# One store per output block, transfers gated on other transfers, and a planner that models the load queue: a change to a fused attention and feed-forward kernel

## The chip, the cores and the metric

The kernel runs on one core of one Trainium2 chip. The time is the device time of one execution in microseconds, and I quote the median of several executions with the lowest and the highest. A profile is one such execution with every instruction recorded. TensorE does the matmuls, VectorE, ScalarE and GpSimd the work between them, and SyncE does nothing here but hand transfers to the DMA engines: "the queue" below is the line of transfers that SyncE hands over, in the order of its list. A weight load and a matmul overlap (in the kernel before they are busy for 153.9 and 218.2 us of a span of 232.9), and the busy time of an engine is time in which at least one of its instructions is recorded.

## The reference

Attention over 4 batches of 768 tokens with 8 heads of 64 (a local band of 96 keys and 8 global keys, a distance bias and a softmax), and a feed-forward on its 3072 x 512 result.

```python
scores = scale * np.matmul(q, k.transpose(0, 1, 3, 2))       # q, k, v: (4, 8, 768, 64) f32
keep = is_global | is_local                                  # 8 global keys, 96 local ones
scores = np.where(keep, scores + bias[None, :, :, :], -1e9)
a = softmax(scores)                                          # shortened
x = np.matmul(a, v).transpose(0, 2, 1, 3).reshape(3072, 512)
h = x @ w_in                                                 # 512 x 2048
g = np.maximum(h, 0.0) + np.log1p(np.exp(-np.abs(h)))        # softplus
out = g @ w_out                                              # 2048 x 512
```

## The kernel before

The 3072 tokens are 24 blocks of 128, in 12 windows of 256. A window is loaded, cast to bf16, and transposed for the scores. Each block gives an attention result `xs`, which is transposed into `XT`. A group of the feed-forward is one window: its first layer (`mm1`) needs the `XT` of both its blocks, ScalarE computes exp and then ln (softplus) into `g`, and its second layer (`mm2`) sums into `o_ps`, is copied to an output buffer `osb` by VectorE and stored.

Every operation is given to a small planner. It simulates the engines with the durations written in the code and fixes the order of the instructions on each engine before the kernel is built. An engine then runs its list in order, whatever really happens: in the trace of the kernel before, VectorE stands 6.06 us before a cast that starts at 101.02, and the copy behind it in the list, whose matmuls started at 97.39 and took 1.04 us, starts at 102.78.

The layout of tokens is where the change begins. A partition p of a loaded tile holds the tokens 2p and 2p+1, so that its two tokens are one piece of 512 bytes in each head. A block therefore comes out with its even tokens first and its odd ones after. The store has to put that right:

```python
def store(g, ns):
    osb = state["osb", g, ns]
    t0 = W * g + P * ns
    dst = out[t0 : t0 + P, :].rearrange("(p r) c -> r p c", r=2)
    for r in range(2):
        nc.sync.dma_start(dst[r], osb[64 * r : 64 * r + 64, :])      # even rows, odd rows

def softplus_ln(g, c):
    gt = tile_of(ffn, ("g", g), [P, NFB, W], BF16)
    nc.scalar.activation(
        gt[:, 4 * c : 4 * c + 4, :].rearrange("p a t -> p (a t)"),
        state["e", g, c][:].rearrange("p a t -> p (a t)"),
        AF.Ln,
        bias=1.0,
    )
```

The first transfers are held back by gates, so that what is needed first gets the DMA engines: a gate is a tiny copy that reads the last bytes of an earlier transfer. Loads of windows 4 and later wait for a matmul group instead.

```python
    load_rest(1, -180.0)
    gate = pool_gate(1, -171.0)          # GpSimd: after k of window 1
    add_weights(0, -170.0, gate)         # w_in and w_out, first quarter
    add_weights(1, -169.0, gate)
    chain = sp_gate(1, -160.0)           # queue: after the second quarter of w_in
    load_rest(2, -150.0)
    gate = pool_gate(2, -149.1)
    add_weights(2, -149.0, gate)
    add_weights(3, -148.0, gate)
    chain = sp_gate(3, -145.0)           # queue: after the fourth quarter of w_in
    for w in range(3, NWIN):
        load_rest(w, base(2 * w) - 14.0)
    # ... cut ...
    for w in range(4, NWIN):
        for what, p in (("q", 0), ("k", 0), ("v", 2)):
            for o in loaded[w, what]:
                o.wait_for(mm1s[w - 3, p])
```

The first blocks are transposed into `XT` by TensorE, the others by a transposing DMA on the same queue:

```python
        if n < 6 or n // 2 == NGRP - 1:
            t = pl.add(f"TX{n}", "pe", 0.23, lambda op: x_transp(n, tr_bank(op.taken)), ...)
            # ... the copy out of PSUM, on VectorE or ScalarE
        else:
            xdone[n] = pl.add(f"DX{n}", "sp", 1.2, lambda op: x_dma(n), u - 20.0, ...)
```

The softmax here doesn't subtract the row's maximum and nothing guards it: scores larger than these inputs give would overflow.

## Time and profile before

| | before |
|---|---|
| time | 232.75 us (231.75 to 233.35, the 3 runs known when the prediction was written) |
| span of the profiled run | 232.9 us |
| TensorE busy | 218.2 us (94%) |
| TensorE idle | 14.7 us, of it 2.3 at the start |
| ScalarE busy | 156.7 us (67%) |
| granted clock at 70 to 80 / 100 to 110 us | 0.83 / 0.66 |
| stores of the loop on the queue | 45, of 128 KB |

TensorE is nearly full, so time is won only from its gaps and from the stretches in which its clock is lowered. The prediction shows where these are. What it tells of the queue ahead of the first gap is read from the timeline of the queue. The columns are start, duration, engine, line, kind, what is written and read, and the count:

```profile
44.60 0.70 SPq L278 DMA_DIRECT2D q_830<-in_q_dram  x1
...
49.02 1.68 SPq L278 DMA_DIRECT2D k_877<-in_k_dram  x1
50.79 1.69 SPq L278 DMA_DIRECT2D v_891<-in_v_dram  x1
...
71.30 1.21 SPq L476 DMA_TRANSPOSE XT<-xs  x1
...
74.50 3.78 SPq L560 DMA_DIRECT2D out_dram<-osb  x6
78.33 0.59 SPq L278 DMA_DIRECT2D q_1295<-in_q_dram  x1
```

The load at 44.60 takes 0.70 us to hand over, those at 49.02 and 50.79, right behind other loads, 1.68 and 1.69 us. The transpose that TensorE is waiting for leaves at 71.30; six half stores then take 3.78 us, and the load of q of window 6 leaves only after them, at 78.33.

### The profile page before, as it was taken

To read this page: it belongs to the slowest core of one execution; us is meant where nothing else is said; L and a number is where in the kernel's file an instruction comes from. 1 tells how busy PE (TensorE), PEld (TensorE's weight loads), DVE (VectorE), ACT (ScalarE), POOL (GpSimd) and SP (SyncE) were. 2 spreads that over 40 slices of the span, in tenths; PEclk is the share of its full clock that TensorE was granted. 3 is DMA by queue.
4 is the path that set the end of the run, shared out by engine and by line. 5 is a ranking of instruction groups with operands and counts; after the bars stand their busy time and mean duration, and the time that the engine had idled before them with its cause. 6 is when DMAs were issued, how large, how long until landed. Compare 5 with 4: busy or idle time off the path is not lost.

```text
span 232.9 us, 5214 instructions
## 1 busy us (share of the span) xinstructions
PE 218.2 (94%) x2131; PEld 153.9 (66%) x2131; DVE 120.2 (52%) x251; ACT 156.7 (67%) x209; POOL 56.5 (24%) x111
## 2 busy tenths in 40 slices
PE   6999997999995998949999999999999999999984
PEld 6887765777754765625676677766676766676643
DVE  6474546659773667151664684555457446310120
ACT  4656477886973777734867877796788778677600
POOL 3471031005820425035035062080260000000000
PEclk9999999999999799976999999999999999999999
DMA  6979899999955896695497595895995112101112
GB/s 164 300 140 193 159 232 178 188 293 291 233 83 100 275 233 147 102 293 112 114 255 139 152 253 102 232 190 103 307 111 114 25 45 48 44 4 45 45 46 91
DMA packets 71849, 35.99 MB, mean 155 GB/s; under 512 B 27665, under 2 KB 68881, under 8 KB 71825
## 3 DMA queue, kind: packets, MB, share of 16 engines
q1 hardware_dynamic: 67456, 31.34, 61.1%
q0 software_dynamic: 4224, 4.19, 11.5%
q8 instruction: 16, 0.26, 0.5%
q10 hardware_dynamic: 144, 0.13, 0.2%
q14 instruction: 9, 0.07, 0.1%
HBM read 27.26 MB, written 6.29 MB: 144 GB/s over the span
## 4 chain that ended last, share of the span: by engine, by line
PE 90%; DVE 4%; DMA 3%; issue 1%; POOL 1%; SPq 0%; POOLq 0%; DVEq 0%
PE o_ps L509 30%; PE h_ps_83 L486 19%; PE h_ps_82 L486 17%; PE x_ps L438 4%; PE o_ps L632 4%; PE s_ps_79 L385 3%; PE s_ps_80 L509 3%; DMA q_1545<-in_q_dram 2%; PE s_ps_80 L385 2%; PE o_ps L534 2%; DMA XT<-xs 1%; PE h_ps_82 L311 1%; DVE z L416 1%; DVE osb L553 1%; PE s_ps_80 L534 1%; PE s_ps_79 L534 1%
## 5 line engine op out<-in xcount | busy, mean ns | idle before, releaser
L486 PEld LDWEIGHTS <-w_in_bf 128*128 128x128 bf16 x768 | 74.9, 99 | 25.1 <-DMA XT<-xs 2.8
L509 PE MATMUL o_ps<-w_out_bf,g 128*128 128x512 bf16 x320 | 83.3, 386 | 4.1 <-DVE osb L553 4.1
L486 PE MATMUL h_ps_83<-XT,w_in_bf 128*128 128x256 bf16 x400 | 52.9, 276 | 0.0
L486 PE MATMUL h_ps_82<-XT,w_in_bf 128*128 128x256 bf16 x368 | 49.5, 279 | 2.7 <-DMA XT<-xs 2.7
L509 PEld LDWEIGHTS <-g 128*128 128x128 bf16 x352 | 32.0, 99 | 29.9 <-issue 5.7
L500 ACT ACTIVATE g<-e 128x1024 bf16<-128x1024 f32 x48 | 50.7, 1056 | 1.2
L496 ACT ACTIVATE e<-h_ps_83 128x512 f32<-128x512 f32 x50 | 29.8, 595 | 28.7 <-PE h_ps_83 L486 28.7
L422 ACT ACTIVATE pb<-z 128x1024 bf16<-128x1024 f32 (+1 forms) x40 | 39.5, 987 | 12.6 <-DVE z L416 12.4
L449 DVE RECIPROCAL rcp<-x_ps 128x4 f32<-128x4 f32 x48 | 8.7, 181 | 51.4 <-PE x_ps L438 40.4
L496 ACT ACTIVATE e<-h_ps_82 128x512 f32<-128x512 f32 x46 | 27.2, 591 | 11.3 <-PE h_ps_82 L486 11.1
L416 DVE TENSOR_TENSOR z<-s_ps_79,biasA 128x1024 f32<-128x1024 f32 x19 | 23.1, 1218 | 3.2 <-PE s_ps_79 L385 3.2
L553 DVE COPY osb<-o_ps 128x512 f32<-128x512 f32 x20 | 13.7, 685 | 18.5 <-PE o_ps L509 18.3
L450 DVE TENSOR_TENSOR xs<-x_ps,rcp 128x256 bf16<-128x256 f32 x48 | 20.4, 424 | 1.9 <-DVE rcp L449 0.2
L416 DVE TENSOR_TENSOR z<-s_ps_80,biasA 128x1024 f32<-128x1024 f32 x15 | 18.3, 1222 | 0.3
L438 PEld LDWEIGHTS <-pb 128*128 128x128 bf16 x320 | 15.0, 98 | 4.5
L632 PE MATMUL o_ps<-ident 128*128 128x128 bf16 x147 | 13.6, 244 | 2.3 <-POOL ident masks.py:199 2.3
L385 PEld LDWEIGHTS <-kT 64*128 64x128 bf16 x352 | 10.0, 94 | 5.2 <-issue 3.4
L632 PEld LDWEIGHTS <-ident 128*128 128x128 bf16 x147 | 10.9, 111 | 3.5 <-POOL ident masks.py:199 2.3
L354 POOL COPY kT<-kT 128x32 bf16<-128x32 bf16 x16 | 3.4, 210 | 35.8 <-PE s_ps_80 L385 18.8
L385 PE MATMUL s_ps_79<-qT,kT 64*128 64x128 bf16 x196 | 10.2, 219 | 1.3 <-DVE z L416 1.3
L509 PE MATMUL s_ps_80<-w_out_bf,g 128*128 128x512 bf16 x32 | 8.2, 379 | 0.0
L385 PE MATMUL s_ps_80<-qT,kT 64*128 64x128 bf16 x156 | 7.9, 216 | 0.0
(125 smaller groups left out, 174.1 us busy)
## 6 DMA issues: line engine op xcount, KB each, us to landing
out_dram<-osb SPq DMA_DIRECT2D x45, 128.0 KB, 2.5
w_in_bf<-in_moe_w_in_dram POOLq DMA_DIRECT2D x4, 512.0 KB, 7.6
w_out_bf<-in_moe_w_out_dram POOLq DMA_DIRECT2D x4, 512.0 KB, 10.3
q_122<-in_q_dram SPq DMA_DIRECT2D x2, 256.0 KB, 4.0
k_124<-in_k_dram SPq DMA_DIRECT2D x2, 256.0 KB, 4.3
v_128<-in_v_dram SPq DMA_DIRECT2D x1, 512.0 KB, 6.6
q_134<-in_q_dram SPq DMA_DIRECT2D x1, 512.0 KB, 7.8
k_146<-in_k_dram SPq DMA_DIRECT2D x1, 512.0 KB, 7.2
```

The costliest lines, as they stand in the source:

```text
L385: nc.tensor.matmul(s_t[:, 4 * sub + (lh // 2 if i == 0 else 2 * (lh // 2) + b), :], k_of(n - b, rows, m), q_of(n, rows, m), start=begin, s ...
L416: nc.vector.tensor_tensor(packed(n, z), rows_of(n, s_t), bias, ALU.add)
L422: nc.scalar.activation(pb[:, 0:nr, :], z[:, 0:nr, :], AF.Exp, scale=1.0 / root_d)
L438: nc.tensor.matmul(xv[:, lh, :], pb[:, 2 * j + b, :], vb_of(n - b)[:, h, :], start=b == 0, stop=b == 1,)
L450: nc.vector.tensor_tensor(xs[:, 4 * half : 4 * half + 4, :], xv[:, :, 0:D], rcp[:][:, :, None].to_broadcast([P, 4, D]), ALU.mult,)
L486: nc.tensor.matmul(hv[:, j, :], w_in_bf[:, m, fb * P : fb * P + P], XT[:, m, W * g : W * g + W], start=(m == 0), stop=(m == NM - 1),)
L496: nc.scalar.activation(e[:, p % 2, :], state["h", g, p][:], AF.Exp)
L500: nc.scalar.activation(gt[:, 4 * c : 4 * c + 4, :].rearrange("p a t -> p (a t)"), state["e", g, c][:].rearrange("p a t -> p (a t)"), AF.Ln ...
L509: nc.tensor.matmul(dst, state["g", g][:, fb, ns * P : ns * P + P], w_out_bf[:, fb, :], start=(fb == 0), stop=(fb == NFB - 1),)
L534: nc.tensor.matmul(bank_of(x)[:, 0 : cols.stop - cols.start], state["g", NGRP - 1][:, fb, ns * P : ns * P + P], w_out_bf[:, fb, cols], sta ...
L553: copy_on[eng](osb[:], src)
L632: nc.tensor.matmul(o_ps[:, 0:P], ident[:], ident[:])
```

## The change

Intent: ln writes `g` so that tokens come out of the second layer in natural order, and a block of output is one store of 128 partitions. The gates of the early loads move to transfers that land sooner. The planner learns how many bytes' worth of transfers stand in the queue and hands over no more while the backlog is large. Blocks 6 and 7 are transposed on TensorE, and three smaller things move.

```diff
     def softplus_ln(g, c):
-            gt[:, 4 * c : 4 * c + 4, :].rearrange("p a t -> p (a t)"),
-            state["e", g, c][:].rearrange("p a t -> p (a t)"),
+            gt[:, 4 * c : 4 * c + 4, :].rearrange("p a (n t r) -> p (a n) r t", n=2, r=2),
+            state["e", g, c][:].rearrange("p b (m r t) -> p (b m) r t", r=2, t=64),
     def store(g, ns):
-        dst = out[t0 : t0 + P, :].rearrange("(p r) c -> r p c", r=2)
-        for r in range(2):
-            nc.sync.dma_start(dst[r], osb[64 * r : 64 * r + 64, :])
+        nc.sync.dma_start(out[t0 : t0 + P, :], osb[:])
     # x_out: the last group's own undoing of the order goes (cut)
     # gates
-    gate = pool_gate(1, -171.0)
+    gate = pool_gate(1, "q", -171.0)
-    chain = sp_gate(1, -160.0)
+    chain = sp_gate("out", 0, -160.0)
-    gate = pool_gate(2, -149.1)
+    gate = pool_gate(2, "k", -149.1)
-    chain = sp_gate(3, -145.0)
+    chain = sp_gate("out", 2, -145.0)
     # transposes of blocks 6 and 7
-        if n < 6 or n // 2 == NGRP - 1:
+        if n < 8 or n // 2 == NGRP - 1:
     # planner: backlog of the queue
-                if free_at[e] > now:
+                if free_at[e] > now or e == "sp" and self.backlog() > 130.0:
     # gate of the loads of windows 4 and later
-                o.wait_for(mm1s[w - 3, p])
+                o.wait_for(mm2s[w - 4, p])
     # banks of the last block's parts
     LAST = (
-        (0, slice(0, DM), ("O", 0)),
-        (1, slice(0, DM // 2), ("S0", 0)),
-        (1, slice(DM // 2, DM), ("S1", 0)),
+        (0, slice(0, DM), ("S0", 0)),
+        (1, slice(0, DM // 2), ("S1", 0)),
+        (1, slice(DM // 2, DM), ("O", 0)),
     )
     # planned durations: store 1.15 -> 0.6, transposing DMA 1.2 -> 1.3; the rest is cut
```

More of the change, by code (lines that the diff above doesn't have):

```diff
@@ L50, in __init__ @@
         self.filler, self.filler_until = filler, filler_until
-        self.moving, self.moved = {"sp": [], "pool": []}, 0.0
+        self.moving, self.moved, self.issued = {"sp": [], "pool": []}, 0.0, 0.0
     def add(self, *args, **kw):
@@ L102, in move, with backlog @@
             self.at(t, lambda: self.move(t))
+    def backlog(self):
+        return self.issued + sum(m[1] for m in self.moving["sp"])
     def arrive(self, now, e, op):
         self.move(now)
+        if e == "sp":
+            self.issued -= op.dma[0]
         self.moving[e].append([op, *op.dma])
@@ L173, in plan @@
                 else:
+                    if e == "sp":
+                        self.issued += op.dma[0]
                     first = now + 1.3 if e == "sp" else op.end + 1.2
@@ L468, in x_out @@
         src = psum[:, 0:512].rearrange("p (m t) -> p m t", m=NPAIR)
-        if n // 2 == NGRP - 1:
-            dst = dst.rearrange("p m (t r) -> p m r t", r=2)
-            src = src.rearrange("p m (r t) -> p m r t", r=2)
         copy_on[eng](dst, src)
@@ L574, in w_out_slice, with after_weights, after_tokens @@
         )
-    def after_weights(s):
-        c = DFF // NS * s
-        nc.sync.dma_start(mark[:, s, :], w_in_bf[0:1, NM - 1, c : c + 16])
-    def after_k(w):
-        nc.gpsimd.tensor_copy(seen[:, w, :], raw_of("k", w)[0:1, H - 1, 0:4])
+    def after_weights(side, s):
+        if side == "in":
+            src = w_in_bf[0:1, NM - 1, DFF // NS * s : DFF // NS * s + 16]
+        else:
+            src = w_out_bf[0:1, NFB // NS * s + NFB // NS - 1, 0:16]
+        nc.sync.dma_start(mark[:, s, :], src)
+    def after_tokens(w, what):
+        nc.gpsimd.tensor_copy(seen[:, w, :], raw_of(what, w)[0:1, H - 1, 0:4])
     rel = const.tile([P, 2, P], F32, name="rel")
@@ L677, in add_weights, with pool_gate, sp_gate @@
         )
-    def pool_gate(w, rank):
-        return pl.add(f"k{w}in", "pool", 0.2, lambda op: after_k(w), rank, after=loaded[w, "k"])
-    def sp_gate(s, rank):
+    def pool_gate(w, what, rank):
         return pl.add(
-            f"w{s}in", "sp", 0.6, lambda op: after_weights(s), rank, after=[landed_in[s]]
+            f"{what}{w}in", "pool", 0.2, lambda op: after_tokens(w, what), rank,
+            after=loaded[w, what],
+        )
+    def sp_gate(side, s, rank):
+        return pl.add(
+            f"w{side}{s}", "sp", 0.6, lambda op: after_weights(side, s), rank,
+            after=[(landed_in if side == "in" else landed_out)[s]],
         )
@@ L744, in attention_window @@
                 else:
-                  c = casts[w, what, part] = pl.add(
-                    f"cast{what}{w}", eng, 0,
-                    lambda op, what=what, hs=hs: cast(op.on, w, what, hs),
-                    u - (5.0 if w < T_DMA else 9.0) + 0.1 * (what == "k"),
-                    after=loaded[w, what] if w else [loaded[w, what][part]],
-                    takes=((what + "b",),) if part == 0 else (),
-                    frees=[(loaded[w, what][0], what + "32")] if part == last else (),
-                )
-                c = c if isinstance(c, list) else [c]
+                    c = casts[w, what, part] = pl.add(
+                        f"cast{what}{w}", eng, 0,
+                        lambda op, what=what, hs=hs: cast(op.on, w, what, hs),
+                        u - (5.0 if w < T_DMA else 9.0) + 0.1 * (what == "k"),
+                        after=loaded[w, what] if w else [loaded[w, what][part]],
+                        takes=((what + "b",),) if part == 0 else (),
+                        frees=[(loaded[w, what][0], what + "32")] if part == last else (),
+                    )
+                    c = [c]
                 wait = [*c, *(done if what == "k" else ())]
@@ L760, in attention_window @@
                         o = pl.add(
-                            f"D{what}{w}", "sp", 1.2,
+                            f"D{what}{w}", "sp", 1.3,
                             lambda op, what=what, i=i: transp_dma(w, what, i), u - 19.0,
@@ L894, in attention_block @@
             xdone[n] = pl.add(
-                f"DX{n}", "sp", 1.2, lambda op: x_dma(n), u - 20.0, after=both,
+                f"DX{n}", "sp", 1.3, lambda op: x_dma(n), u - 20.0, after=both,
                 frees=[(norm[n, 0], "xs")], dma=(32, 20), slack=2.0,
@@ L973 @@
             pl.add(
-                f"store{g}_{ns}", "sp", 1.15, lambda op, g=g, ns=ns: store(g, ns), r + 3.0,
+                f"store{g}_{ns}", "sp", 0.6, lambda op, g=g, ns=ns: store(g, ns), r + 3.0,
                 after=[oc], frees=[(oc, "osb")], dma=(8, 145),
```

## The prediction

> **What bounds the kernel now.** I read the page first, then the waits of TensorE, then a table of stretches, then the timelines around the two worst stretches. TensorE is busy almost throughout:
>
> ```profile
> span 232.9 us, 5214 instructions
> ...
> PE 218.2 (94%) x2131; PEld 153.9 (66%) x2131; DVE 120.2 (52%) x251; ACT 156.7 (67%) x209; POOL 56.5 (24%) x111
> ...
> PE   6999997999995998949999999999999999999984
> ...
> PEclk9999999999999799976999999999999999999999
> ```
>
> So 14.7 us of TensorE are idle, and the clock row has two dips, at slices 14 and 18 to 19 (5.8 us each), where the PE row dips as well. Where nothing is missing, a group of eight first-layer matmuls takes 0.87 us on the chain that ended last and a group of four second-layer ones 0.86 us. Outside the dips the time is therefore the sum of the matmuls, and only gaps can be won. The waits of TensorE name them:
>
> ```profile
> PE o_ps L509 <- DVE osb L553: 4.1, 2, 3.3
> PE h_ps_82 L486 <- DMA XT<-xs: 2.7, 1, 2.7
> PE o_ps L632 <- POOL ident masks.py:199: 2.3, 1, 2.3
> PE s_ps_79 L385 <- DVE z L416: 1.3, 1, 1.3
> PE o_ps L534 <- DVE osb L553: 0.8, 1, 0.8
> ```
>
> The columns are total us, times, longest. The 2.3 us is the start and stays. The table of stretches shows that the large two cost more than their idle time:
>
> ```profile
> 70.00:80.00 10.00, 7.33 (x76) 5.37 (x75) 5.05 (x11) 4.67 (x7) 1.62 (x4) 0.83 0.68 185
> 100.00:110.00 10.00, 6.67 (x31) 3.51 (x30) 3.61 (x8) 3.89 (x6) 4.89 (x8) 0.66 0.84 187
> 110.00:200.00 90.00, 90.00 (x879) 62.90 (x877) 52.06 (x98) 69.24 (x90) 21.24 (x40) 1.00 0.69 143
> ```
>
> The third number from the right is the granted clock: after each gap it falls, while the 90 us that follow run at 1.00 with no gap at all. Why the second gap exists is in the timelines of the load queue and of VectorE:
>
> ```profile
> 90.37 2.56 SPq L333 DMA_TRANSPOSE kT<-kb  x2
> 93.02 1.18 SPq L560 DMA_DIRECT2D out_dram<-osb  x2
> 94.30 1.25 SPq L476 DMA_TRANSPOSE XT<-xs  x1
> 95.61 1.56 SPq L278 DMA_DIRECT2D q_1545<-in_q_dram  x1
> ```
>
> ```profile
> 101.02 0.69 DVE L285 CAST qb<-q_1545 128x1024 bf16<-128x1024 f32 x1 [6.06 <-DMA q_1545<-in_q_dram]
> ...
> 102.78 0.68 DVE L553 COPY osb<-o_ps 128x512 f32<-128x512 f32 x1
> ```
>
> The queue issues back to back, so the load of window 7 leaves at 95.6 and lands 5.4 us later. VectorE, in order, has the cast of that load ahead of the copy that frees o_ps; it sits 6.06 us and TensorE runs dry. The first gap is the same queue: the transpose XT<-xs that TensorE needs at 71 is issued only at 71.30, behind loads that took about 1.7 us each to issue between 49 and 56, two store halves (3.5 us) and four transposes of q and k with 1.2 us or more each.
>
> [...] second-layer groups after the second gap take 1.86 and 1.71 us instead of 0.86[...] The trace has the cost of the split: two halves take 1.18 us of the issuing queue when it is free, about 0.59 each. [...]
>
> **The change, part by part.**
>
> *Store in one piece.* 22 pairs of half stores become 22 stores; each saves about 0.59 us of the queue, 13 us over the run. It is worth nothing where the queue is idle (after 110 us), and moves what is behind it earlier in the congested part (44 to 98 us), where some seven pairs lie: about 4 us or more, as a pair took 3.5 us behind a backlog.
>
> *Blocks 6 and 7 transposed on TensorE.* Two transposes of 1.2 us leave the queue, and the first gap's wait (mm1 of group 3 needs blocks 6 and 7) has no DMA left in it. Cost: eight more matmuls (2138 against 2131, with one filler less), 0.23 us a block, +0.5 us.
>
> *Gates.* Weights wait for q of window 1 rather than k, 1.8 us earlier by the two landings (11.2 and 12.9 us); the loads of windows 2 and 3 wait for the first w_out of a pair rather than the second w_in, one 0.5 MB slice earlier, some 2.6 us at the 200 GB/s of that stretch. Before, the DMA engines stand nearly idle at 13 to 15 and 26 to 28 us. By window 3 these add to an estimated 5 to 7 us (its loads left at 44.6). That gives the queue slack in the stretch of both gaps.
>
> *Backlog in the planner, load of w after mm2 of w-4.* In the built order loads and transposes now alternate, instead of eight loads in a row at 44.6 to 56. TensorE's order is nearly the same: block 12's scores come after 36 first-layer and 27 second-layer groups in both. The new gate of window 7 is second-layer group 25, which ends about 3.7 us of matmuls before the last probability product ahead of block 12. The load needs 4.4 to 5.4 us, and its cast still stands before the copy of o_ps in VectorE's order. I work out a VectorE lag of 1 to 2 us there against about 0.9 us of slack: a rest of perhaps 0.5 us at block 12 and again at block 18. After blocks 14, 16 and 20 the order has three first-layer groups ahead of the copy, which cover it.
>
> *ln writes g with a step of two.* 48 instructions:
>
> ```profile
> L500 ACT ACTIVATE g<-e 128x1024 bf16<-128x1024 f32 x48 | 50.7, 1056 | 1.2
> ...
> L326 ACT COPY kT<-h_ps_82 128x512 bf16<-128x512 bf16 x4 | 2.1, 589 | 1.1 <-PE h_ps_82 L311 1.1
> ...
> L473 ACT COPY XT<-s_ps_79 128x512 bf16<-128x512 bf16 x1 | 0.7, 736 | 0.6 <-PE h_ps_83 L486 0.6
> ```
>
> The last line is the only write of ScalarE with a step of two in this kernel, 147 ns longer than the same size without it (512 elements). If that scales, ln costs 1.35 us rather than 1.06: 48 x 0.29 = 14 us, ScalarE from 156.7 to about 171 us (73%). In 110 to 200 it is idle 23% and an ln is followed by 0.2 to 1.1 us of idle time, so the most is hidden; between 40 and 70 it is 84% busy (25.1 of 30 us) and would come near 91% with its 8 of them. I take +0.5 us.
>
> *End.* The last block's first part moves from o_ps, which waited 0.8 us for a copy, to a free bank: -0.8 us.
>
> **Sum.** Gap at 71: 2.7 us and the lost clock, (1 - 0.83) x 10 = 1.7: -4.4. Gap at 100: 3.3 us, and on the chain 1.86 + 1.71 + 1.71 + 1.01 for four groups of 0.86 or 0.87, 2.8: -6.1. The smaller o_ps wait (0.8), half: -0.4. The z wait at 37 us (one first-layer and one second-layer group now stand between the two scores): -1.3. End: -0.8. Transposes +0.5, rests at blocks 12 and 18 +1.0, ln +0.5, and +1.5 for waits that a new order makes and I can't name: 232.75 - 13.0 + 3.5 = 223.25 us. I say 223.5.
>
> **Rivals.** (a) The gap moves: after the first is gone TensorE reaches block 12 some 6 us sooner and asks the queue that much sooner. For it: XT of block 9 now stands behind both transposes of q and a store, and I have only 2 to 3 us of slack for it. Against: the earlier gates (5 to 7), the stores (4) and the two transposes (2.4) add to 12 us. With one gap of that kind left the time would be about 228. (b) ScalarE becomes the bound in 40 to 70 us through the slower ln: at most 8 x 0.29 = 2.3 us, time about 225.5. Against it: the first-layer groups run ahead of the second layer by a whole group. (c) All gaps close and nothing new comes: 220. (d) The queue was hidden anyway and only the order matters: same as now, 231 to 233; speaks against it that two waits with their clock account for 10.5 us.
>
> **Range and chances.** The sum without allowances is 220.3, with one gap of the second kind kept some 228. Range 219.8 to 228.5. The 2% line is 228.1; the gap at 71 and the end give 5.2 - 0.5 us on their own, nearly that. Faster 0.82, same 0.16, slower 0.02.
>
> **What would show it.** Right: no wait on XT<-xs and at most 1 us waits on osb between 60 and 110 us, granted clock 1.00 there, half as many stores, loads of window 3 leaving before 40 us, TensorE busy about 213 us and idle under 10. ln at 1.2 to 1.35 us with no TensorE wait on ScalarE. Wrong: a wait of 2 us or more on a load, an XT transpose or osb with a clock dip after it; ScalarE near full with TensorE waiting for it; window 3 loads still at 44 us.

## The result, and the profile after

| | before | after |
|---|---|---|
| median (lowest to highest), 4 runs each | 232.86 us (231.75 to 233.35) | 223.56 us (223.32 to 223.88) |
| ratio of the fast runs | | 0.9608, interval 0.9571 to 0.9644 |
| span of the profiled run | 232.9 us | 222.1 us |

A run counts as slow when it takes over 1.5% more than the fastest of the same kernel beside it. All four runs of the kernel after are recorded as fast, and the four before lie within 0.7% of each other. A ratio is the mean time of one kernel's fast runs over that of the other's fast runs of the same rounds, so it is not quite the ratio of the medians beside it. The kernel became 9.3 us faster, against 9.25 predicted.

The page of the kernel after, with busy times and shares, and then the busy tenths and the granted clock in 40 slices of the span:

```profile
span 222.1 us, 5201 instructions
...
PE 213.9 (96%) x2138; PEld 152.3 (69%) x2138; DVE 120.3 (54%) x253; ACT 167.0 (75%) x208; POOL 57.7 (26%) x112
...
PE   5999989999996999999999999999999999999994
...
PEclk9999999999999999999999999999999999999999
```

The clock row has no dip left. The difference of the two spans is 10.8 us, more than the 9.3 us of the medians, since the profiled run before (234.69 us) was slower than those of the table. TensorE is busy 4.3 us less (218.2 to 213.9), although it does seven matmuls more, and idle 6.5 us less (14.7 to 8.2). I put the 4.3 us, two fifths of this difference, down to the clock, 0.83 and 0.66 in the two stretches before and 1.00 after (an estimate); no list of waits shows it. What is left of the waits of TensorE (total us, times, longest):

```profile
PE o_ps L637 <- POOL ident masks.py:199: 2.3, 1, 2.3
PE o_ps L513 <- DVE osb L557: 1.1, 1, 1.1
PE h_ps_83 L489 <- ACT XT L476: 0.7, 1, 0.7
PE h_ps_82 L489 <- DVE XT L476: 0.6, 1, 0.6
PE h_ps_83 L489 <- DVE XT L476: 0.2, 1, 0.2
```

And the table of stretches of the kernel after (stretch, its length, then busy time and instructions of TensorE, of its weight loads, of VectorE, ScalarE and GpSimd, then clock, DMA share and GB/s):

```profile
70.00:80.00 10.00, 8.87 (x94) 6.25 (x93) 7.53 (x15) 7.22 (x9) 3.71 (x9) 1.00 1.12 254
...
100.00:110.00 10.00, 10.00 (x108) 6.91 (x106) 4.86 (x9) 7.60 (x10) 1.58 (x5) 1.00 0.76 204
110.00:200.00 90.00, 90.00 (x846) 63.08 (x845) 50.51 (x93) 73.31 (x90) 20.99 (x39) 1.00 0.58 127
```

Both bad stretches run at a granted clock of 1.00, and 1.13 us is missing in the first, which is the one osb wait above. The queue's timeline after has the three loads that matter, of q of windows 3, 6 and 7:

```profile
39.84 0.52 SPq L285 DMA_DIRECT2D q_794<-in_q_dram  x1
...
68.68 2.77 SPq L562 DMA_DIRECT2D out_dram<-osb  x3
71.50 0.43 SPq L285 DMA_DIRECT2D q_1281<-in_q_dram  x1
...
88.38 0.43 SPq L285 DMA_DIRECT2D q_1555<-in_q_dram  x1
```

They left at 44.60, 78.33 and 95.61 before: 4.8, 6.8 and 7.2 us earlier now. The lead grows along the queue; three stores take 2.77 us where three pairs took 3.78. Not all of this lead is the queue's own: in the code before, the load of window 6 also waits for the first `mm1` of group 3, and that is the matmul which the first gap held until 73.77. So through this gate a gap of TensorE can hold back a load that a later matmul needs. VectorE then has the cast of window 7 and the copy behind it early enough, and one copy that was late for another reason:

```profile
70.40 0.69 DVE L557 COPY osb<-o_ps 128x512 f32<-128x512 f32 x1 [2.08 <-DMA out_dram<-osb]
...
92.84 0.69 DVE L292 CAST qb<-q_1555 128x1024 bf16<-128x1024 f32 x1 [2.24 <-DMA q_1555<-in_q_dram]
...
94.97 0.69 DVE L557 COPY osb<-o_ps 128x512 f32<-128x512 f32 x1
```

In brackets is the idle time of VectorE and what ended it. The cast still waits for its load, but only 2.24 us rather than 6.06, and the copy at 94.97 keeps no matmul waiting. The copy at 70.40 waited for an output buffer that a store behind the queue freed late: that is the osb wait of 1.1 us.

ScalarE, the row of ln (busy us, mean ns, idle before), and its timeline at the place where the first gap was:

```profile
L504 ACT ACTIVATE g<-e 128x1024 bf16<-128x1024 f32 x48 | 64.8, 1350 | 1.0
```

```profile
66.25 1.35 ACT L504 ACTIVATE g<-e 128x1024 bf16<-128x1024 f32 x1
67.47 0.55 ACT L476 COPY XT<-h_ps_82 128x512 bf16<-128x512 bf16 x1
```

An ln takes 1350 ns instead of 1056. The copy of block 7 into `XT`, which took the place of the transposing DMA, stands behind it, and the first-layer group at 68.08 waits 0.74 us for it.

### The profile page after: what moved, and what is told of

Its sections match the earlier page's. It is cut to its first block, busy times and chain, and to the rows that moved or that the text cites. A ratio compares the mean times of both kernels' runs of the same rounds, so it can differ in the third digit from the quotient of the medians.

```text
span 222.1 us, 5201 instructions
## 1 busy us (share of the span) xinstructions
PE 213.9 (96%) x2138; PEld 152.3 (69%) x2138; DVE 120.3 (54%) x253; ACT 167.0 (75%) x208; POOL 57.7 (26%) x112
## 4 chain that ended last, share of the span: by engine, by line
PE 87%; DMA 5%; DVE 4%; SPq 1%; issue 1%; POOL 1%; DVEq 0%; POOLq 0%
PE o_ps L513 29%; PE h_ps_83 L489 18%; PE h_ps_82 L489 17%; PE o_ps L637 5%; PE x_ps L445 4%; PE s_ps_79 L392 3%; DMA out_dram<-osb 3%; PE s_ps_80 L513 3%; DMA q_1281<-in_q_dram 2%; PE s_ps_80 L392 2%; PE s_ps_79 L538 2%; PE h_ps_82 L318 1%; DVE osb L557 1%; PE o_ps L538 1%; PE s_ps_80 L538 1%; PE s_ps_79 L377 1%
## 5 line engine op out<-in xcount | busy, mean ns | idle before, releaser
L489 PEld LDWEIGHTS <-w_in_bf 128*128 128x128 bf16 x768 | 73.8, 98 | 22.4 <-DVE XT L476 1.2
L513 PE MATMUL o_ps<-w_out_bf,g 128*128 128x512 bf16 x320 | 82.3, 380 | 1.1 <-DVE osb L557 1.1
L504 ACT ACTIVATE g<-e 128x1024 bf16<-128x1024 f32 x48 | 64.8, 1350 | 1.0
L489 PE MATMUL h_ps_83<-XT,w_in_bf 128*128 128x256 bf16 x392 | 50.8, 273 | 1.0 <-ACT XT L476 0.7
L489 PE MATMUL h_ps_82<-XT,w_in_bf 128*128 128x256 bf16 x376 | 48.8, 273 | 0.6 <-DVE XT L476 0.6
L637 PEld LDWEIGHTS <-ident 128*128 128x128 bf16 x146 | 10.4, 110 | 3.4 <-POOL ident masks.py:199 2.3
```

The source lines that it names most:

```text
L489: nc.tensor.matmul(hv[:, j, :], w_in_bf[:, m, fb * P : fb * P + P], XT[:, m, W * g : W * g + W], start=(m == 0), stop=(m == NM - 1),)
L504: nc.scalar.activation(gt[:, 4 * c : 4 * c + 4, :].rearrange("p a (n t r) -> p (a n) r t", n=2, r=2), state["e", g, c][:].rearrange("p b ( ...
L513: nc.tensor.matmul(dst, state["g", g][:, fb, ns * P : ns * P + P], w_out_bf[:, fb, :], start=(fb == 0), stop=(fb == NFB - 1),)
L637: nc.tensor.matmul(o_ps[:, 0:P], ident[:], ident[:])
```

## The experiments

Two theories. **Lateness**: the queue is late as a whole between 44 and 98 us. Every part of the change that moves it earlier buys slack, the two gaps are two places where the same lateness shows, and taking out one part brings a gap back somewhere. **Separate causes**: the first gap belongs to the two transposing DMAs, the second to stores and gates, and each part is worth its own sum. A third possibility is that the new order of the planner (backlog, gate of the loads) did it. Beside these, the cost of the slower ln was to be measured.

All ratios are against the kernel before, run on the same chip in the same job: 233.79 us (232.59 to 236.0) in the first job (e1 to e4), 234.04 (230.21 to 236.06) in the second (e5 to e8), 233.16 (230.64 to 237.15) in the third (e9 to e12). The kernel before itself varies by 3%, more than the kernel after. Medians are of all runs, ratios of the fast ones.

One caution holds for all of these. Only e3, e5, e6 and e7 keep the planned order of the kernel after. In the others the planner makes a new order from the edit, so a part is tested together with the order that it brings.

### One part out of the kernel after

**e1_tx6**: blocks 6 and 7 again by DMA.

```diff
-        if n < 8 or n // 2 == NGRP - 1:
+        if n < 6 or n // 2 == NGRP - 1:
```

> The changed kernel with blocks 6 and 7 transposed by DMA again (eight TensorE transposes fewer, 0.5 us of matmuls). Theory 'queue slack' (the earlier loads, the shorter stores and the alternating order all give the in-order load queue time, and the two gaps were only lateness of that queue): the XT transpose of block 7 now leaves around 66 us and lands around 68.5 us, about when TensorE asks for it, so a wait of 0 to 1.5 us without a clock dip: 223 to 225 us. Rival 'TX' (taking these two transposes off the queue is what closed the gap at 71 us): a wait on XT<-xs of 2 us or more with a clock dip, 226 to 228 us.

Measured: 227.08 us (226.28 to 227.34), ratio 0.970 (0.9635 to 0.9765). Its waits of TensorE:

```profile
PE o_ps L513 <- DVE osb L557: 2.7, 2, 1.6
...
PE h_ps L489 <- DMA XT<-xs: 0.4, 1, 0.4
```

The wait for the transpose did not come back at 2.7 us but at 0.4, since the queue is earlier by the other parts: the transpose leaves at 67.65 instead of 71.30. The loss sits elsewhere: q of window 6 leaves at 76.92 instead of 71.50, and o_ps waits. By its time the run falls into the range of the rival 'TX' (226 to 228), by its waits it does not: both theories had it partly wrong. That the loss moves rather than returns speaks for lateness.

**e2_gates**: the old gates.

```diff
-    gate = pool_gate(1, "q", -171.0)
+    gate = pool_gate(1, "k", -171.0)
-    chain = sp_gate("out", 0, -160.0)
+    chain = sp_gate("in", 1, -160.0)
-    chain = sp_gate("out", 2, -145.0)
+    chain = sp_gate("in", 3, -145.0)
```

> The changed kernel with the old gates of the early loads (weights after k of window 1, windows 2 and 3 after the second w_in of each pair). Queue slack: the loads of window 3 leave near 44 us again instead of 39.8, the slack of some 5 us is gone and a gap of 1 to 4 us comes back between 65 and 105 us: 225 to 229 us. Rival 'gates are hidden' (TensorE is never short of early data): 223.2 to 224.2 us, with loads of window 3 at 44 us and no new wait.

Measured: 228.0 us (226.41 to 229.37), ratio 0.9742 (0.9656 to 0.9829). The loads of window 3 leave at 45.74, q of window 6 at 79.94, and the waits are

```profile
PE s_ps L392 <- DVE z L423: 2.4, 2, 1.7
PE o_ps L513 <- DVE osb L557: 2.3, 1, 2.3
```

with the clock at 0.95 and 0.94 in the stretches 70 to 80 and 80 to 100 us. The time is in the range of queue slack. A gate that opens 6 us later at 40 us is still felt at 80, but not all of the loss is that: 1.67 of the 2.4 us on z (the scores with their bias, on VectorE) end at 38.85, before the loads of window 3 leave at all. The kernel before has 1.32 us of this wait at 38.06, and e10, with the early gates, has none. So the gates also earn a sum of their own, ahead of the crowded queue.

**e3_split**: half stores again, and with them the contiguous ln and the last group's own undoing of the order. On every engine the order of the plan is that of the kernel after.

```diff
-        nc.sync.dma_start(out[t0 : t0 + P, :], osb[:])
+        dst = out[t0 : t0 + P, :].rearrange("(p r) c -> r p c", r=2)
+        for r in range(2):
+            nc.sync.dma_start(dst[r], osb[64 * r : 64 * r + 64, :])
     # and softplus_ln and x_out as in the kernel before
```

> The changed kernel with each store as two halves of 64 partitions and g written contiguously by ln, in the same planned order of every engine (the planner still believes in one store). Queue slack: some seven more issues of 0.6 us before 100 us, 2 to 4 us of lateness, of which part reaches TensorE: 224 to 226.5 us. Rival 'stores hidden': 223 to 223.8 us. Rival 'ln costs' (the slower ln of 1.35 us holds TensorE): under 222.8 us, as ln is back at 1.06 us.

Measured: 227.53 us (226.88 to 229.6), ratio 0.974 (0.9661 to 0.9818). Its queue at the critical place:

```profile
71.57 3.79 SPq L567 DMA_DIRECT2D out_dram<-osb  x6
75.41 0.59 SPq L285 DMA_DIRECT2D q<-in_q_dram  x1
```

Three pairs take 3.79 us, the load of window 6 leaves 3.9 us later than in the kernel after, and TensorE waits 4.3 us for osb in four places, with the clock at 0.83 in 70 to 80 us. ScalarE is 10.8 us less busy in this kernel (156.2 against 167.0 us) and it is slower all the same: the stores are worth more than the cheaper ln. The time is above all three expected ranges. Two things overstate what the stores are worth in the stretch of the gaps: the profiled run is the slowest of the four, the other three having a mean clock of 0.998 to 1.0, and three of the four osb waits, 1.75 us in sum, come at 117 to 150 us, where the kernel before has no gap. The planned order of e3 counts on one short store. But since this order is that of the kernel after, e3 is the run that shows best that the queue matters and not only the order.

**e4_nobacklog**: the planner's limit on the backlog taken away.

```diff
-                if free_at[e] > now or e == "sp" and self.backlog() > 130.0:
+                if free_at[e] > now or e == "sp" and self.backlog() > 1e9:
```

> The changed kernel with the planner's limit on the queue's backlog taken away: eight loads stand in a row before the first transposes again. Queue slack: the first qT transposes leave near 60 us instead of 54.5, TensorE is late at block 8 or the transposes of x for groups 4 and 5, 1 to 5 us: 224.5 to 228.5 us. Rival 'order does not matter once the loads are early': 223 to 224.2 us.

Measured: 224.89 us (224.46 to 225.28), ratio 0.9618 (0.9543 to 0.9692), which is the kernel after within its interval. Its time is just inside the range of queue slack (224.5 to 228.5), but the waits of 1 to 5 us that this foresaw did not come: the longest on osb is 0.7 us. The planner's model of the backlog is not needed for most of the gain; whether it is worth a few tenths of a per cent is not resolved. In this job e4 is also the best stand-in for the kernel after, and e1 to e3 are 2.2 to 3.1 us above it.

### Measuring ln and the output buffer

**e5_after**: the kernel after, unedited, for the second job.

> The changed kernel unedited, as the mark for the runs beside it and for the first four runs, whose kernel before took 233.8 us on their chip against 232.9 us earlier. All theories: ratio to before 0.957 to 0.965.

Measured: 223.33 us (222.73 to 227.5; the last is a slow run), ratio 0.955 (0.9499 to 0.96), a little below the expected 0.957 to 0.965.

**e6_lnflat**: ln contiguous and nothing else. The output rows come out in the wrong order on purpose, so the result is wrong (relative error 0.024).

```diff
-            gt[:, 4 * c : 4 * c + 4, :].rearrange("p a (n t r) -> p (a n) r t", n=2, r=2),
-            state["e", g, c][:].rearrange("p b (m r t) -> p (b m) r t", r=2, t=64),
+            gt[:, 4 * c : 4 * c + 4, :].rearrange("p a t -> p (a t)"),
+            state["e", g, c][:].rearrange("p a t -> p (a t)"),
```

> The changed kernel with ln writing g contiguously and nothing else changed: same plan, same instructions, the output rows of each block in a wrong order on purpose (a wrong result). Theory 'ln is mostly hidden': ln at 1.06 us, ScalarE 14 us less busy, the 0.7 us wait of TensorE on the XT copy that ScalarE makes behind two ln at 64 to 67 us goes, the time falls by 0.5 to 1.0 us. Rival 'ScalarE bounds the stretch of 40 to 70 us': falls by 2 us or more. Rival 'wholly hidden': within 0.3 us of the changed kernel.

Measured: 223.38 us (222.45 to 226.01, one slow run), ratio 0.9554 (0.9497 to 0.961). The row of ln:

```profile
L504 ACT ACTIVATE g<-e 128x1024 bf16<-128x1024 f32 x48 | 50.7, 1055 | 1.1
```

The write with a step of two costs 295 ns an instruction and 11.3 us of ScalarE's busy time (167.0 against 155.7; the row's sum differs by 14.1, and I did not follow up the rest beyond seeing that neighbouring records overlap by some 0.1 us, as the timeline of ScalarE above shows). The edit also makes one run of 1024 elements out of the runs of 64 into which both sides were cut, so the step and the short runs are measured together. Of the time, it costs nothing that six runs resolve: the expected 0.5 to 1.0 us did not come, and the rival 'wholly hidden' holds.

**e7_osb4**: a fourth output buffer, in a pool of its own; the order on every engine is unchanged.

```diff
+    outp = ctx.enter_context(tc.tile_pool(name="outp", bufs=4))
-        osb = tile_of(ffn, ("osb", g, ns), [P, DM], F32)
+        osb = tile_of(outp, ("osb", g, ns), [P, DM], F32)
     # the last block's osb likewise; the planner's "osb": 3 -> 4
```

> The changed kernel with four output buffers in place of three; the planned order stays the same on every engine. Theory 'the rest wait at 70 us is a store late in the queue' (the copy of o_ps waits until a store has emptied its buffer): the copy at 70.4 us starts right after its matmuls at 67.2 us, the wait of 1.1 us goes, the time falls by 0.8 to 1.3 us. Rival 'VectorE is late for another reason, the cast of a late load': no change, within 0.3 us.

Measured: 223.15 us (222.47 to 223.52), ratio 0.9538 (0.9489 to 0.9588). Of its stretches:

```profile
70.00:80.00 10.00, 10.00 (x101) 6.95 (x100) 7.90 (x17) 8.71 (x12) 4.87 (x10) 1.00 1.38 276
```

TensorE is busy all 10 us, and the osb wait is gone from its list. The copy now starts at 68.22. So the reading of the copy at 70.40 is confirmed. The expected gain of 0.8 to 1.3 us did not come: in time it is within the noise of e5.

### One part into the kernel before

**e8_b_tx8**: the two transposes alone.

```diff
-        if n < 6 or n // 2 == NGRP - 1:
+        if n < 8 or n // 2 == NGRP - 1:
```

> The kernel before with only blocks 6 and 7 transposed on TensorE. If the two gaps are separate (gap at 71 us closes, gap at 100 us stays): 4.4 us less and 0.5 us more than before, 228.5 to 230 us, ratio 0.98 to 0.99. Queue slack as one thing (what is not waited for at 71 is waited for later in the same late queue): the gap at 71 us goes, another one of 2 us or more comes on the loads of window 6 or 7 or on their cast, 230 to 233 us, ratio 0.985 to 1.0.

Measured: 232.22 us over 22 runs (227.36 to 233.36), fast runs alone 0.9858 (0.9808 to 0.9908). Most runs, the profiled one too, count as slow, being over 1.5% above the fastest. The five fast ones have a median of 229.09 us and a mean clock of 0.982 to 0.992, below the 0.998 to 1.0 of the first four runs of the kernel after. Their time and ratio fit separate causes (228.5 to 230, 0.98 to 0.99) at least as well as lateness (230 to 233, 0.985 to 1.0). The trace shows what happens in a slow execution, and not what the fast ones do:

```profile
PE x_ps L438 <- DVE xs L450: 5.9, 1, 5.9
```

The gap of 2.7 us at 71 is gone, and one of 5.9 us ends at 84.92, behind the cast of q of window 6, ahead of which VectorE stands idle for 5.71 us until 83.62; the trace names nothing that ended this idle time, but q of window 6 had left at 77.06. In this execution the gap moved, as rival (a) of the prediction has it.

**e10_b_gates**: the early gates alone (the load gates and the planner as before).

```diff
-    gate = pool_gate(1, -171.0)                  # after k of window 1
+    gate = <the same copy, after q of window 1>
-        nc.sync.dma_start(mark[:, s, :], w_in_bf[0:1, NM - 1, c : c + 16])
+        nc.sync.dma_start(mark[:, s, :], w_out_bf[0:1, NFB // NS * s + NFB // NS - 1, 0:16])
-    chain = sp_gate(1, -160.0)                   # after landed_in
+    chain = sp_gate(0, -160.0)                   # after landed_out
-    chain = sp_gate(3, -145.0)
+    chain = sp_gate(2, -145.0)
```

> The kernel before with the earlier gates of the early loads only. Rival 'the gates alone do it' (loads of window 3 leave near 40 us, 5 us earlier, which is more than either gap): 224 to 226 us. Queue slack with all parts needed: one gap stays or moves, 227 to 231 us.

Measured: 229.99 us (228.35 to 231.3), ratio 0.9866 (0.9804 to 0.9929), all four runs fast enough to count. The profiled run is a fast one. The loads of window 3 leave at 39.62, and no matmul waits for a transpose XT<-xs any more, although blocks 6 and 7 still go by DMA. The second gap is there with 2.03 us, ending at 100.18, and a new one stands before it:

```profile
PE x_ps L438 <- DVE vb L363: 3.5, 1, 3.5
PE o_ps L509 <- DVE osb L553: 2.4, 2, 2.0
```

The lines of VectorE and TensorE show the chain from the load to the matmul:

```profile
82.30 0.69 DVE L285 CAST qb<-q 128x1024 bf16<-128x1024 f32 x1 [4.18 <-DMA q<-in_q_dram]
82.91 0.60 DVE L363 COPY vb<-vb 4x512 bf16<-4x512 bf16 x2
...
83.56 0.37 PE L438 MATMUL x_ps<-vb,pb 128*128 128x65 bf16 x7 [3.48 <-DVE vb L363]
```

The load of q of window 6 left at 76.80; VectorE had its cast at the head of its list and stood for 4.18 us, the small copy behind it was late, and TensorE waited 3.48 us for that copy. The list of waits names the copy; the cause is two instructions further back.

**e9_b_three**: the two transposes, the early gates and the natural order with one store, in the kernel before; no backlog in the planner, the old gate of the loads, the old last banks.

```diff
     # e8_b_tx8 and e10_b_gates together, and softplus_ln, store and x_out of the kernel after
-                f"store{g}_{ns}", "sp", 1.15, lambda op, g=g, ns=ns: store(g, ns), r + 3.0,
+                f"store{g}_{ns}", "sp", 0.6, lambda op, g=g, ns=ns: store(g, ns), r + 3.0,
```

> The kernel before with three parts of the change only: blocks 6 and 7 transposed on TensorE, the earlier gates of the early loads, and ln in token order with one store. Left out: the planner's backlog, the later gate of the loads from window 4 on, the other bank for the last block. Theory 'queue slack from these three is enough': both gaps and the clock dips go, the 0.8 us wait at the end stays: 223.5 to 225.5 us. Rival 'the planner's backlog model or the later load gate is needed': a gap of 2 us or more between 65 and 105 us stays, 226 us or more.

Measured: 223.26 us (222.72 to 224.25), ratio 0.9575 (0.9535 to 0.9616): the whole gain, a little below the expected 223.5 to 225.5. Its waits include no DMA and no osb wait over 0.8 us, and q of window 6 leaves at 71.11:

```profile
PE o_ps L530 <- DVE osb L549: 0.8, 1, 0.8
PE x_ps L438 <- DVE xs L450: 0.8, 1, 0.8
...
71.11 0.57 SPq L278 DMA_DIRECT2D q<-in_q_dram  x1
```

### The rest

**e11_last**: the last block's banks as before.

```diff
-        (0, slice(0, DM), ("S0", 0)),
-        (1, slice(0, DM // 2), ("S1", 0)),
-        (1, slice(DM // 2, DM), ("O", 0)),
+        (0, slice(0, DM), ("O", 0)),
+        (1, slice(0, DM // 2), ("S0", 0)),
+        (1, slice(DM // 2, DM), ("S1", 0)),
```

> The changed kernel with the banks of the last block as before (first part in o_ps). All theories: only the end moves, a wait of 0.8 us of TensorE on the copy of o_ps comes back, 0.6 to 1.0 us more than the changed kernel; as a rival, no change if the end is bound by the last store and not by TensorE.

Measured: 224.67 us (223.78 to 225.7), ratio 0.9632 (0.9589 to 0.9676). The wait is back as a line,

```profile
PE o_ps L538 <- DVE osb L557: 0.8, 1, 0.8
```

and the time agrees with 0.8 us within its noise. The kernel after was not run in this job, and e9, which has the old banks and the same wait, took 223.26 us, so the cost in time is not shown.

**e12_best**: the kernel after with the four output buffers of e7 and the planner told that an ln takes 1.35 us.

```diff
-                    f"sln{g}_{p // 2}", "act", 1.06,
+                    f"sln{g}_{p // 2}", "act", 1.35,
     # and the edit of e7_osb4
```

> An attempt at a better version: the changed kernel with four output buffers and with the planner told that ln takes 1.35 us, so that it plans around the slower ln. If the waits left at 66 to 70 us (0.7 for the XT copy, 1.0 for the buffer) both go and the new order brings no other: 221.5 to 223 us against 223.3 for the changed kernel. Rival: the plan was already good enough and the new order costs as much as it saves: 223 to 224.5 us.

Measured: 222.84 us (222.16 to 223.6), ratio 0.9553 (0.9518 to 0.9587). It is the lowest median of all, but its interval overlaps those of e5 and e9, and it is not shown to beat the kernel after.

### The runs together

| kernel | q of window 6 leaves at | q of window 7 | TensorE busy in 70 to 110 us (of 40) | clock there | median us |
|---|---|---|---|---|---|
| before | 78.33 | 95.61 | 33.20 | 0.87 | 232.86 |
| e8, transposes alone (slow profile) | 77.06 | 92.15 | 34.14 | 0.91 | 232.22 (fast runs 229.09) |
| e10, gates alone | 76.80 | 92.75 | 33.80 | 1.00 | 229.99 |
| e2, without the gates | 79.94 | 94.26 | 36.43 | 0.96 | 228.0 |
| e3, without one store | 75.41 | 92.59 | 36.73 | 0.96 | 227.53 |
| e1, without the transposes | 76.92 | 91.25 | 36.70 | 1.00 | 227.08 |
| e4, without the backlog | 69.80 | 86.51 | 38.54 | 1.00 | 224.89 |
| after | 71.50 | 88.38 | 38.82 | 1.00 | 223.56 |
| e9, the three parts | 71.11 | 85.80 | 39.42 | 1.00 | 223.26 |
| e7, four output buffers | 69.80 | 87.00 | 40.00 | 1.00 | 223.15 |

The medians are from different jobs, so small differences between rows mean nothing. Some traces also miss matmuls (e3 has 2105 of 2138), which counts as idle time: in e10 a group that shows three matmuls in place of four has 0.16 us of it ahead, at 87.50 and again at 95.59.

The kernels fall into two classes. Where the load of window 6 leaves by 71.5 us, TensorE loses at most 1.5 us of the 40; where it leaves after 75, it loses 3.3 us or more. Two of the three parts, with the rest of the change around them, leave 3.3 to 3.6 us missing. Between 71.5 and 75 there is no kernel. Within the late class the time does not follow the departure: e2 leaves last and takes 228.0 us, e10 leaves 3 us sooner and takes 229.99.

What is shown is that the three parts are enough (e9) and that each is needed: in one job, every run of e1, e2 and e3 is slower than every run of e4. That they act through one late queue is read from the traces; the times do not force it. In their fast runs e8 and e10 gain 1.4% and 1.3% alone, and e3, which has both these parts and no single store, gains 2.6%. So the two add up within the intervals, as separate causes would have it. What speaks for one lateness is where the waits are. Without the transposes on TensorE, e1 does not get its old gap of 2.7 us back, only 0.4, and waits 1.60 us for an output buffer and 1.14 us behind the cast of window 7 instead. The gates alone, in e10, take away the wait on the transpose without touching the transposes, leave 2.03 us of the second gap, and bring a new gap of 3.48 us behind the load of window 6. And e3 gets a gap and a late load with the order of every engine unchanged. Part of what the gates are worth, the z wait of 1.3 to 1.7 us at 38, is a cause of its own. The new order of the planner is not needed (e4, e9).

Left open: the single store was never run alone in the kernel before, and the three parts in pairs are known only with the rest of the change around them (e1 to e3). Where the fast runs of e8 lose their time is not profiled. The gate of the loads was never taken alone; it is not needed, but whether it helps is not shown. And two other ways to natural order without the stepped ln, in the read of the first layer's matmul or in the read of the exp, were built but not run; putting it into the second layer's weight load does not build.

## Why the prediction was right

The time, the range and the class held. The idea of one late queue held too, but several steps were right in size for another reason, and that the errors cancelled is luck. Two readings were slightly off: the first dip of the PE row is in slice 13, one ahead of the clock's, and ahead of the transpose at 71.30 stand seven transposes of q and k and one of xs since 59.72, not four. By its steps:

- **Gap at 71, -4.4.** Right: no wait on the transpose, clock 1.00. But the step credited the two transposes alone, and that was too narrow: e1 without them has only 0.4 us of that wait, e10 without them has none, and e8 with them alone has a gap later in its slow profile. They were one of three contributions to one queue.
- **Gap at 100, -6.1.** Right: the cast at 92.84 waits 2.24 us rather than 6.06, and no matmul waits behind it.
- **Rests at blocks 12 and 18, +1.0, and the halved o_ps wait, -0.4.** The size was right, the place and the cause were not. Nothing waits at block 12. The 1.1 us that is left lies at 71 and comes from an output buffer; e7 takes it away. The prediction counted casts and had not looked at when a store gives its buffer back.
- **z wait, -1.3.** Gone, with one first-layer and one second-layer group between the two scores, as said. But the step stood apart from the gates, and it is they that bring it: e2 with the old gates has the wait again (1.67), with nothing between the two scores, and e10 with the early gates alone has none. **End, -0.8.** The wait is gone, and e11 brings it back as the same 0.8.
- **Transposes, +0.5.** Seven more matmuls, 2138, as said.
- **ln, +0.5.** The duration was right to the digit, 1.35 us, scaled from a single copy of 736 ns. In part that is luck: the same copy without the step takes 567 ns in the kernel after, not 589, and would have given 1.39. ScalarE came to 167.0 us, not 171, and of the +0.5 us e6 shows nothing in the time. The prediction also said that no wait of TensorE on ScalarE would be seen; there is one of 0.7 us, for the copy of block 7 that stands behind an ln. With the contiguous ln of e6 that wait is still 0.5, so it belongs to the moved transpose more than to ln.
- **Waits it could not name, +1.5.** The copies of `XT` out of PSUM are these: 0.7, 0.6 and 0.2 on the list of waits, 1.5 in sum. That the sum agrees is luck. Only the 0.7 comes with the moved transposes and could have been named; the 0.6 lies at 29 us and is in e10 too, where only the gates move, and the 0.2 at 54 us is in e1 too, where the transposes are not moved.
- **Queue lead of 5 to 7 us by window 3.** Measured 4.8 (44.60 to 39.84), a little under. Behind it the lead grew to 6.8 and 7.2 us at windows 6 and 7, in part because the first gap, which had held a matmul that the loads wait for, was gone.
- **Signs.** Busy 213.9 against 213 said, idle 8.2 against under 10, half as many stores (45 to 23 on the queue), window 3 before 40: all met. "At most 1 us" on osb was missed by 0.1.
- **Rivals.** (a) is real as a mechanism, as e10 shows in a fast run and e8 in a slow one, and (b) and (c) did not come: TensorE keeps 29.01 of 30 us in 40 to 70 with ScalarE at 26.44. (d) falls with the time itself, and with e3, which keeps the new order, splits the stores and is 2.6 us slower than e4.

## What to carry to other kernels

When several waits of a saturated engine lead back to one in-order queue, treat them as one lateness: ask at what time the next needed transfer leaves, and expect that a single repair may move the gap rather than close it, until the whole queue is early enough. Here the early gates alone (e10) took away the wait of 2.7 us on the transpose and brought one of 3.48 us behind the load of window 6. Test parts both by leaving one out and by putting one in, and look where the waits are then: here the times of two parts add up, and only the places of the waits show that the gaps hang together. And when an engine in order holds a cast of a load ahead of a copy that frees another engine, the list of waits names the copy, so follow that engine's timeline back to the load: in e10 it names the copy with 3.48 us, and the 4.18 us before the cast show the load.

## What else the traces show

- A bf16 write with a step of two on ScalarE: ln took 1350 ns instead of 1055 for 1024 elements a partition (the kernel after against e6), about 0.29 ns an element, unless it is the runs of 64 elements that cost, which e6 takes away as well.
- The gap and the clock: in the kernel before, a gap of 2.67 us was followed by a clock of 0.83 over 70 to 80 us; in e10 one of 3.48 us left it at 1.00 over 80 to 100 us. So in these runs the length of a gap alone does not tell whether the clock falls. After the gap of 2.67 us, which ended at 73.77, a first group of eight matmuls still took 1.05 us; the slow ones, 1.78 and 1.91 us, started at 74.90.
- How long a hand-over holds the queue: in the kernel after 0.43 us for the loads of 512 KB at 71.50 and 88.38, each behind a store, and 0.52 us for the one at 39.84; in the kernel before 1.53 to 1.69 us for the five loads from 47.38 to 54.4, each right behind another load; once 4.41 us (v of window 3 in the kernel after, at 41.09); and 1.2 us or more for a transpose. Since 512 KB in 1.7 us are some 310 GB/s, close to the 291 to 293 GB/s that the page of the kernel before shows for 46 to 58 us, the long ones may be the pace of the data and not a cost of the hand-over (an estimate, not tested).
